# Two chunks of a delta-rule recurrence inverted one by one instead of as a pair, with a new order of all instructions

## The chip, the cores and the metric

The kernel runs on one core of one Trainium2 chip. Its time is the device time of one execution, in microseconds (us); before the change the median of three executions is 238.32 us (238.15 to 238.89). Five engines work side by side, each through its own queue in order: TensorE (PE, matmul), VectorE (DVE), ScalarE (ACT), GpSimd (POOL) and SyncE (SP, which only issues DMAs here). They meet at semaphores.

## The reference

Four batches of eight heads run a gated delta rule over 768 steps with 48 features; its output, 3072 tokens of 384 features, goes through a dense layer of 2048, a softplus and a second dense layer back to 384.

```python
q, k, v, beta, g                       # (4, 8, 768, 48); beta (4, 8, 768)
k_n = k / (norm(k, axis=-1) + 1e-6)
for t in range(768):                   # state (4, 8, 48, 48), zero at first
    y[t] = g[t] * (q[t] @ state)
    state += beta[t] * outer(k_n[t], v[t] - k_n[t] @ state)
x = y.transpose(0, 2, 1, 3).reshape(3072, 384)
out = softplus(x @ w_in) @ w_out       # w_in (384, 2048), w_out (2048, 384)
```

## The kernel before

**Tiling.** The 768 steps are cut into 12 chunks of 64. Within a chunk the recurrence is solved in matrix form: with the gram matrix of the chunk's keys and beta a triangular matrix of 64 by 64 is made for each of the 32 heads, inverted, and the state goes from chunk to chunk by a few matmuls. Chunk by chunk there are these stages, each an *item* of the program:

- load k, q, v, g (SP, in two halves of 192 KB each); square and sum the keys (ksq, red), take the root (sqrt for chunks 0 to 3, pow on GpSimd for the others), scale or cast the keys (kmul, cast), transpose them on TensorE (trs) and evict them (kev, qev);
- gram matrices on TensorE (gram; gramd makes only the diagonal blocks), evicted as kk (kkc, kd) and, masked, as mt (mask);
- the *inversion* of the diagonal blocks (below), then its *join*: xmm, xs, tmm, td2 and zmm make the inverse of the whole 64 by 64 matrix out of the inverses of the 16 by 16 blocks;
- the *chain*, which carries the state from chunk to chunk: ks (keys times state), w (v minus that), umm, u1, zu, u2, smm, s (the new state), and for the output qs, ymm, y, ytr, xt;
- the *dense* layers: g1 (w_in, L992) with softplus on ScalarE (L1004), then g2 (w_out, L1019), eviction (o) and store. Chunks 0, 1, 10 and 11 are dense one by one with 256 columns to a matmul, the others in pairs with 512.

**The inversion.** Chunks go through it in pairs (GROUPS, [0, 1] to [10, 11]). A transpose on VectorE (ln, L594 or L601) puts one 32 by 32 diagonal block of one head on each of 128 partitions: 32 heads by 2 blocks by 2 chunks are 128 lanes. In each lane two blocks of 16 by 16 are inverted side by side by a product (prep, L641) and 15 steps that depend on each other, each a product (tmp, L661) and a sum (tt, L668) on VectorE or GpSimd. ca and cb put the result into the halves of a masked tile (L683 to L685), and three transposes (st.a, st.c, st.b; L711) bring it back to the layout of the heads in dn, tb and td; tx copies half of tb to the other partitions (L209). For group 0 (DIAGONALS) ln reads the diagonal blocks alone, so it need not wait for the whole gram, but it waits for the keys, norms and blocks of both chunks: lbeta (L577 to L580) makes beta over the square of the norm for the pair at once.

**The order.** Nothing schedules the program: a table written out by hand or by a planner (`_ORDER`) names every item by its number with the engine that runs it, and `emit` goes through it. Each engine runs its items in that order; a buffer of a ring (all PSUM banks are one ring of eight) goes to the item that comes first in the table. Items on an engine that wait hold up all behind them. TensorE has 40 optional *fill* items (four matmuls on the identity, L1049) that the table may place, and places 12 times.

**Before the items** the program makes constants: the identity, masks mk and mx, tiles filled with zero or fixed blocks, and GpSimd issues four small DMAs that bring beta of chunks 0 and 1 lane by lane into beta_l (L179).

## Time and profile before

| What | Value |
|---|---|
| median of three executions | 238.32 us (238.15 to 238.89) |
| the profiled execution, its own time | 240.57 us |
| its span, first to last instruction | 238.9 us |
| mean granted clock of TensorE | 0.941 |
| TensorE busy | 217.7 us (91%) |
| VectorE, ScalarE, GpSimd busy | 170.6, 146.8, 114.7 us |
| read from and written to HBM | 25.26 MB, 4.72 MB |

Lines of timelines read: start and length in us, engine, line of the kernel, operation, output<-input without buffer numbers, shapes, the count of instructions merged into the row, and in brackets the idle time before it with what ended it. Lines of stretches read: the stretch, its length, then for TensorE, its weight loads, VectorE, ScalarE and GpSimd the busy us with the number of instructions, then the granted clock, the busy share of the DMA engines and GB/s; with one line of the kernel picked, TensorE's matmuls and weight loads alone. A busy TensorE is not one at its peak, because matmuls are pipelined and their ends are modelled.

### The profile page before, as it was taken

What the parts mean: (1) busy time and instruction counts of PE and PEld (TensorE: products, weight loads), DVE (VectorE), ACT (ScalarE), POOL (GpSimd) and SP (SyncE); (2) the same over time, 40 slices, a digit from 0 to 9 for tenths busy, and PEclk for the clock granted to TensorE, in tenths of its full rate; (3) what the DMA queues carried; (4) which work ended last, traced back from release to release, by engine and by line L of the source; (5) the groups of instructions that cost most, each with busy time, mean ns of one, the idle gap of its engine ahead of it and who ended that gap; (6) DMA issues with size and microseconds to landing.
All of it is one profiled execution on the core that took longest, in us unless ns stands there. A gap on an engine that the chain in (4) does not pass through costs nothing.

```text
span 238.9 us, 11420 instructions
## 1 busy us (share of the span) xinstructions
PE 217.7 (91%) x5016; PEld 141.2 (59%) x5016; DVE 170.6 (71%) x374; ACT 146.8 (61%) x293; POOL 114.7 (48%) x203
## 2 busy tenths in 40 slices
...
PEclk9997955599999958999999999999999999999999
...
GB/s 100 201 210 152 204 130 157 178 187 199 145 144 137 175 180 149 119 136 139 152 164 162 75 79 63 135 139 48 21 20 71 82 69 21 68 22 16 19 53 95
DMA packets 86833, 27.57 MB, mean 115 GB/s; under 512 B 77048, under 2 KB 86776, under 8 KB 86784
## 3 DMA queue, kind: packets, MB, share of 16 engines
...
q0 software_dynamic: 3840, 3.17, 8.8%
...
q14 instruction: 10, 0.08, 0.1%
HBM read 25.26 MB, written 4.72 MB: 126 GB/s over the span
## 4 chain that ended last, share of the span: by engine, by line
PE 72%; POOL 8%; DVE 6%; ACT 5%; issue 4%; DMA 3%; SPq 1%; DVEq 0%; POOLq 0%; ACTq 0%
PE d L992 26%; PE d L1019 22%; PE d L513 3%; PE d L939 3%; DMA f<-in_k_dram 3%; POOL tt L668 3%; PE d L829 2%; PE d L451 2%; POOL tmp L661 2%; PE d L419 2%; PE d L1049 2%; PE d L966 2%; PE d L883 2%; PE d L792 2%; DVE mt L495 2%
## 5 line engine op out<-in xcount | busy, mean ns | idle before, releaser
L1019 PE MATMUL d<-w_out,ga 128*128 128x384 f16 x384 | 70.0, 327 | 0.0
L992 PE MATMUL d<-xt,w_in 128*128 128x512 f16 (+1 forms) x384 | 69.0, 330 | 0.0
L1004 ACT ACTIVATE ga<-d 128x512 f16<-128x512 f32 x96 | 52.8, 604 | 12.7 <-PE d L992 10.8
L992 PEld LDWEIGHTS <-w_in 128*128 128x128 f16 x384 | 35.9, 99 | 22.2 <-issue 0.3
L1019 PEld LDWEIGHTS <-ga 128*128 128x128 f16 x384 | 34.9, 98 | 22.0 <-issue 1.1
L661 POOL TENSOR_TENSOR tmp<-nn,tt 128x78 f32<-128x78 f32 (+7 forms) x58 | 20.6, 356 | 16.3 <-DVE tt L668 12.5
L370 POOL TENSOR_TENSOR nv<-nv,half_c 128x16 f32<-128x16 f32 x8 | 23.5, 2933 | 9.1 <-DVE nv L359 9.0
L668 POOL TENSOR_TENSOR tt<-tt,tmp 128x78 f32<-128x78 f32 (+7 forms) x58 | 22.6, 390 | 4.5
L207 ACT ACTIVATE kqt<-d 128x1024 f16<-128x1024 f16 x18 | 18.3, 1023 | 9.1 <-PE d L451 7.6
L495 DVE TENSOR_TENSOR mt<-d,mask 128x256 f16<-128x256 f32 x48 | 19.0, 414 | 3.3 <-PE d L513 2.9
L207 ACT ACTIVATE osb<-d 128x384 f32<-128x384 f32 x15 | 7.3, 489 | 21.9 <-PE d L1019 21.8
L207 ACT ACTIVATE u<-d 128x384 f16<-128x384 f32 x29 | 13.5, 492 | 11.7 <-PE d L896 5.9
L641 POOL TENSOR_TENSOR nn<-ln,beta_l 128x256 f32<-128x256 f16 x9 | 7.5, 854 | 23.1 <-DVE ln L624 23.0
L953 DVE TENSOR_TENSOR yg<-d,f 128x384 f16<-128x384 f32 x24 | 12.7, 547 | 5.9 <-PE d L939 4.1
L1049 PE MATMUL d<-ident 128*128 128x512 f16 x48 | 14.9, 459 | 1.7 <-DVE ident L195 1.7
L209 DVE CAST u<-d 128x384 f16<-128x384 f32 x19 | 10.2, 552 | 7.3 <-PE d L896 4.0
L209 DVE COPY osb<-d 128x384 f32<-128x384 f32 x9 | 5.0, 552 | 14.0 <-PE d L1019 14.0
L513 PE MATMUL d<-kqt 48*64 48x128 f16 (+1 forms) x448 | 11.6, 229 | 2.8 <-ACT kqt L207 1.3
L869 DVE TENSOR_TENSOR w<-f,d 128x384 f16<-128x384 f32 x22 | 11.3, 539 | 3.1 <-PE d L829 2.7
L927 DVE TENSOR_TENSOR s<-s,d 128x384 f16<-128x384 f16 x20 | 10.7, 547 | 3.0 <-PE d L913 2.9
L209 POOL COPY tx<-tb 64x512 f16<-64x512 f16 x8 | 4.9, 607 | 16.1 <-DVE tb L711 7.4
L359 DVE TENSOR_REDUCE nv<-f 128x16 f32<-128x768 f32 x12 | 11.3, 941 | 1.4 <-POOL f L350 1.4
(117 smaller groups left out, 368.9 us busy)
## 6 DMA issues: line engine op xcount, KB each, us to landing
...
```

The costliest lines, as they stand in the source:

```text
L207: nc.scalar.activation(o, x, AF.Copy, scale=float(sign))
L209: ENG[en].tensor_copy(o, x)
L370: nc.gpsimd.tensor_tensor(nvs(), nvs(), half_c[:, :NU], ALU.pow)
L495: nc.vector.tensor_tensor(mt[c][m].ap[:, NP * p : NP * p + NP], gb[m].ap.rearrange("p (i b) -> p i b", i=NP)[:, :, n : n + C], mask[:, Non ...
L513: nc.tensor.matmul(gb[m].ap.rearrange("p (i b) -> p i b", i=NP)[HALF[r], i, lo:hi], x[:, :C], x[:, lo:hi],)
L661: ENG[en].tensor_tensor(t, nn.ap[:, :, j : j + 1, j + 1 :].broadcast_to([P, 2, w, n]), tt.ap[:, :, :w, j : j + 1].broadcast_to([P, 2, w, n ...
L668: ENG[en].tensor_tensor(rows, rows, t, ALU.add)
L953: lambda en, m=m: nc.vector.tensor_tensor(heads(yg.ap, m), hd(yp[m].ap), heads(gf.ap, m), ALU.mult),
L992: nc.tensor.matmul(hp.ap[:, n * b : n * b + n], w_in[:, j, f * P : (f + 1) * P], xt.ap[:, j, t0 : t0 + n], start=(j == 0), stop=(j == 2),)
L1004: lambda en, hp=hp, o=gb: nc.scalar.activation(o.ap, hp.ap, AF.Softplus),
L1019: nc.tensor.matmul(op.ap[:, :DM], b.ap[:, col + c0 : col + c0 + 128], w_out[:, f, :], start=(f == 0), stop=(f == NF - 1),)
L1049: nc.tensor.matmul(hp.ap, ident, ident[:, None, :].broadcast_to([P, 4, P]))
```

## The change

Group 0 is no longer inverted as a pair. A new function, solo, does it for chunk 0 and again for chunk 1, and a pair's code (inverse) is left to the other five groups; the join is a function of its own that both call. In solo a lane holds one 16 by 16 block of one head: 32 heads by 4 blocks of one chunk are 128 lanes. The transpose (ln1) then moves 256 words instead of 512, a selection (pick1) and a shorter lbeta are added for each chunk, each step's product and sum have half the elements, and there are 30 steps instead of 15. The two halves of a lane's result are masked by mz and mk, the two transposes back (st.a, st.b) have the size they had, the third is gone, and tx copies from td. Beta of chunks 0 and 1 comes in eight DMAs of half the size into beta_s. Each chunk has its own kd (one buffer, so chunk 1's follows chunk 0's) and its own td. Everything else is the same work, but `_ORDER` is written anew for all items, so the place and often the engine of an item differ throughout; 11 fills are placed instead of 12.

```diff
+    mz = pool.tile([P, 2], F32, name="mz")
+    mb = pool.tile([P, 1], F32, name="mb")
+    beta_s = pool.tile([P, 2, 16], F32, name="beta_s")
...
+    r_kd = ring("kd", 1, [P, NU, HC], F16)
...
-            nc.gpsimd.dma_start(
-                out=beta_l[l0 : l0 + 32, 0], in_=bt[:2, :, HC * x : HC * x + HC]
-            )
+            for c in range(2):
+                nc.gpsimd.dma_start(
+                    out=beta_s[l0 : l0 + 32, c],
+                    in_=bt[c, :, HC * x : HC * x + HC].rearrange("u (b k) -> b u k", b=2),
+                )
...
+    def solo(c, cl, kk):
+        nl, bl, nv = Buf(r_nl), Buf(r_bl), nv_of[c]
+        kd, ln, nn, tt, tmp = kd_of[c], Buf(r_ln), Buf(r_n), Buf(r_t), Buf(r_tmp)
...
+        bl_it = add("lbeta", tag, "D", lbeta, deps=[nv_it[c]], bufs=[nv, nl, bl])
...
+        l1 = add("ln1", tag, "D", lnt, deps=kd_it[c], bufs=[kd, ln])
...
+        l1 = add("pick1", tag, "D", pick, deps=[l1], bufs=[ln])
+        prev = add("clear", tag, "GD", lambda en: ENG[en].memset(tt.ap[:, 0], 0.0), bufs=[tt])
...
+        def step(en, j):
+            n, w = 15 - j, j + 1
...
+            t = tmp.ap[:, : n * w].rearrange("p (c i) -> p c i", c=w)
+            ENG[en].tensor_tensor(
+                t,
+                nn.ap[:, 0, j : j + 1, j + 1 :].broadcast_to([P, w, n]),
+                tt.ap[:, 0, :w, j : j + 1].broadcast_to([P, w, n]),
+                ALU.mult,
+            )
+            rows = tt.ap[:, 0, :w, j + 1 :]
+            ENG[en].tensor_tensor(rows, rows, t, ALU.add)
+
+        prev = add("prep", f"{tag}.0", en0, prep, deps=[l1, prev, bl_it], bufs=[ln, nn, bl])
+        for j in range(15):
+            prev = add("step1", f"{tag}.{j}", en0, lambda en, j=j: step(en, j),
+                       deps=[prev], bufs=[nn, tt, tmp], size=(15 - j) * (j + 1))
...
+        ta_it = add("st", f"{tag}.a", "D", lambda en: lanes_out(dn.ap, ta.ap, 0, 1),
+                    deps=ca, bufs=[ta, dn], size=512)
+        td_it = add("st", f"{tag}.b", "D", lambda en: lanes_out(td.ap, rows(), 2, 2),
+                    deps=cb, bufs=[t1, td], size=512)
...
+        if gi in DIAGONALS:
+            for cl, c in enumerate(cs):
+                solo(c, cl, kk_of[gi])
+            return
...
 _ORDER = """
-S25 S26 D227 S34 S33 D6 D11 A176 D173 A9 A1 G169 D170 D0 A171 G5 A197 A12 P129 P152 P164 P132 P162
+S25 S26 A6 A12 G0 G2 G14 G266 G11 G4 A27 A7 A169 D1 D228 D10 D173 S33 S35 S34 D170 P150 P160 P162
```

Three places of the new order, as the instructions stand on their engine (line of that kernel, operation, output<-input with buffer numbers, shape). First GpSimd, around the end of the first inversion; before, the last step of the pair, the copy tx, a weight DMA and the first chain's w:

```order
L661 TENSOR_TENSOR tmp_115<-nn_113,tt_117 128x56
L668 TENSOR_TENSOR tt_117<-tt_117,tmp_115 128x2x14x2
L661 TENSOR_TENSOR tmp_115<-nn_113,tt_117 128x30
L668 TENSOR_TENSOR tt_117<-tt_117,tmp_115 128x2x15
L209 COPY tx_123<-tb_122 64x512
L327 DMA w_in<-in_moe_w_in_dram 128x3x512
L861 TENSOR_TENSOR w_131<-f_76,nv_92 128x384
```

and in the change, from chunk 1's product to the copy tx of chunk 0 (its own last step is three rows above):

```order
L696 TENSOR_TENSOR nn_117<-ln_115,bl_99 128x256
L707 TENSOR_TENSOR tt_120<-nn_117,tt_120 128x15
L712 TENSOR_TENSOR tmp_119<-nn_117,tt_120 128x28
L719 TENSOR_TENSOR tt_120<-tt_120,tmp_119 128x2x14
L712 TENSOR_TENSOR tmp_119<-nn_117,tt_120 128x39
L719 TENSOR_TENSOR tt_120<-tt_120,tmp_119 128x3x13
L712 TENSOR_TENSOR tmp_119<-nn_117,tt_120 128x48
L719 TENSOR_TENSOR tt_120<-tt_120,tmp_119 128x4x12
L712 TENSOR_TENSOR tmp_119<-nn_117,tt_120 128x55
L719 TENSOR_TENSOR tt_120<-tt_120,tmp_119 128x5x11
L217 COPY tx_127<-td_129 64x256
L335 DMA w_in<-in_moe_w_in_dram 128x3x512
```

The copy that the join of chunk 0 needs now follows the first five steps of chunk 1, and the first weight DMA, which stood among the pair's steps, follows the copy.

Second VectorE, around the transpose ln that opens the inversion of chunks 2 and 3 (kk_98 before, kk_101 in the change); before:

```order
L211 TENSOR_SCALAR kk_98<-d_168 128x4x64
L953 TENSOR_TENSOR yg_145<-d_171,f_75 128x8x48
L495 TENSOR_TENSOR mt_111<-d_168,mask 128x256
L953 TENSOR_TENSOR yg_145<-d_174,f_75 128x8x48
L601 STREAM_TRANSPOSE ln_112<-kk_98 128x1024
L380 RECIPROCAL nv_93<-nv_93 128x16
L869 TENSOR_TENSOR w_133<-f_82,d_173 128x384
L869 TENSOR_TENSOR w_131<-f_82,d_174 128x384
```

and in the change (L592 is xs of chunk 1, L217 its td2):

```order
L503 TENSOR_TENSOR mt_114<-d_173,mask 128x256
L367 TENSOR_REDUCE nv_97<-f_84 128x16
L503 TENSOR_TENSOR mt_111<-d_178,mask 128x256
L219 TENSOR_SCALAR kk_101<-d_179 128x4x64
L592 TENSOR_TENSOR xs_128<-d_176,mk 128x16x16
L592 TENSOR_TENSOR xs_128<-d_172,mk 128x16x16
L503 TENSOR_TENSOR mt_114<-d_178,mask 128x256
L217 CAST td_130<-d_174 128x8x2x16
L219 TENSOR_SCALAR kk_101<-d_175 128x4x64
L503 TENSOR_TENSOR mt_113<-d_175,mask 128x256
L797 STREAM_TRANSPOSE ln_115<-kk_101 128x1024
```

The transpose stood ahead of w of chunk 1 and now stands behind that chunk's w, its two transposes back, its xs and its td2.

Third TensorE, in the chain of chunk 2 (zu ends, then smm); before, one of the pieces of the second dense layer stands between:

```order
L896 MATMUL d4_172<-u163_137,z2_130 64x48
L1019 LDWEIGHTS ga9_158
L1019 MATMUL d7_175<-w_out_73,ga9_158 128x384
L1019 LDWEIGHTS ga15_164
L1019 MATMUL d7_175<-w_out_73,ga15_164 128x384
L913 LDWEIGHTS kn2_88
L913 MATMUL d1_169<-u164_138,kn2_88 64x48
```

and in the change zmm of chunk 3 follows zu at once:

```order
L1015 LDWEIGHTS z2_134
L1015 MATMUL d5_177<-u163_141,z2_134 64x48
L1015 LDWEIGHTS z2_134
L1015 MATMUL d6_178<-u162_140,z2_134 64x48
L631 LDWEIGHTS kk1_101
L631 MATMUL d1_173<-td2_131,kk1_101 64x32
```

From xmm of chunk 2 to ytr of chunk 3 there stood eight such pieces, one piece of the first layer and a fill; in the change there are four pieces of the second layer and neither of the others.

396 lines of the change are left out of this document (230 added, 166 removed).

## The prediction

> **What bounds the kernel now.** I read the page's totals first, then a table of busy time in five stretches that I cut at milestones of TensorE, then the chain of waits, and last the timelines of the engines from 0 to 91 us. The page:
>
> ```profile
> span 238.9 us, 11420 instructions
> ...
> PEclk9997955599999958999999999999999999999999
> ```
>
> The granted clock of TensorE is given in 40 slices of 5.97 us: it is down in the first third alone, worst in the sixth to eighth slice (30 to 48 us) and the fifteenth (84 to 90). The stretches (time, then busy us of each engine with its instructions, clock, DMA share, GB/s):
>
> ```profile
> 0.00:44.20 44.20, 31.65 (x795) 20.97 (x796) 37.57 (x97) 31.68 (x61) 26.48 (x50) 0.80 1.01 165
> 44.20:65.60 21.40, 20.84 (x340) 15.73 (x336) 15.69 (x39) 16.52 (x31) 15.65 (x27) 0.94 1.18 178
> 65.60:91.00 25.40, 21.63 (x711) 15.34 (x710) 20.04 (x42) 13.43 (x28) 15.51 (x28) 0.87 0.83 158
> 91.00:235.00 144.00, 143.54 (x3180) 89.19 (x3176) 97.33 (x200) 84.66 (x174) 57.01 (x100) 1.00 0.45 84
> 235.00:238.90 3.90, 0.00 (x0) 0.00 (x0) 0.00 (x0) 0.48 (x1) 0.00 (x0) 0.88 0.38 90
> ```
>
> The cuts are these starts on TensorE: the first dense matmul (chunk 0, 256 columns), the join of chunk 2 (xmm), and the first dense matmul of chunks 2 and 3 (512 columns):
>
> ```profile
> 44.18 1.46 PE L992 MATMUL d<-xt,w_in 128*128 128x256 f16 x6
> 65.61 0.43 PE L741 MATMUL d<-dn,kk 64*64 64x32 f16 x32
> 91.02 4.76 PE L992 MATMUL d<-xt,w_in 128*128 128x512 f16 x21
> ```
>
> From 91.0 to 235.0 TensorE idles 144.00 - 143.54 = 0.46 us at full clock: that stretch is pure work, and the same work after the change. So the kernel's time is the moment M at which chunks 2 and 3 become dense, plus 144.0, plus a tail of 3.9. An edit in the first 91 us is worth what it moves M, and nothing else; starting chunk 0's dense work earlier is worth nothing by itself, because chunks 0 and 1 together hold too little of it to last until M.
>
> **The change, step by step.**
>
> *The inversion of chunk 0.* Now the two chunks are inverted as one pair:
>
> ```profile
> 13.65 0.19 DVE L579 TENSOR_TENSOR bl<-beta_l,nl 128x32 f32<-128x32 f32 x1
> 14.18 1.04 DVE L594 STREAM_TRANSPOSE ln<-dn 128x512 uint32<-128x512 uint32 x1
> 15.26 0.76 DVE L641 TENSOR_TENSOR nn<-ln,bl 128x256 f32<-128x256 f16 x2
> 22.20 0.28 DVE L661 TENSOR_TENSOR tmp<-nn,tt 128x128 f32<-128x128 f32 x1
> ...
> 18.81 0.41 POOL L661 TENSOR_TENSOR tmp<-nn,tt 128x120 f32<-128x120 f32 x1 [2.41 <-DVE tt L668]
> 19.30 0.41 POOL L668 TENSOR_TENSOR tt<-tt,tmp 128x120 f32<-128x120 f32 x1
> 27.50 0.25 POOL L661 TENSOR_TENSOR tmp<-nn,tt 128x30 f32<-128x30 f32 x1
> 27.83 0.26 POOL L668 TENSOR_TENSOR tt<-tt,tmp 128x30 f32<-128x30 f32 x1
> ...
> 1.64 2.65 POOL L179 DMA_DIRECT2D beta_l<-in_beta_dram  x4 [0.27 <-issue]
> beta_l<-in_beta_dram POOLq DMA_DIRECT2D x4, 4.0 KB, 4.8
> ```
>
> The pair's steps end at 27.83 + 0.26 = 28.1. In the change chunk 0 no longer waits for chunk 1's load, but for its beta: the four DMAs cost GpSimd 0.66 us each to issue (2.65 / 4), eight cost 5.3; the seventh is the last that chunk 0 needs, is issued at 1.64 + 6 x 0.66 = 5.6 to 6.3, and lands 4.8 later, at 11. Then two products of 0.19, half a transpose (0.5), the selection (0.4 at most), one product for nn (0.38): 12.6. Step 1 stands on VectorE (0.5 with the hop), the other 13 pairs on GpSimd. Their size halves but not their time: 30 elements cost 0.25 and 120 cost 0.41, so 0.20 + 0.0018 per element; 15 to 64 elements cost 0.285 on average, and the two rows at 18.81 and 19.30 stand 0.49 apart, 0.08 more than the first lasts. 26 x (0.285 + 0.08) = 9.5. **End 23.1 instead of 28.1: -5.0.** A bound from below: on VectorE a full-sized one is 0.28, so nothing on the chip makes these steps much shorter than that; from above: GpSimd's full cost, 26 x 0.49 = 12.7, end 26.3.
>
> *From there to the first dense matmul.* 28.1 to 44.2 is 16.1 us now. Two rows of GpSimd (a copy tx that the join needs, and two products for nn):
>
> ```profile
> 31.66 0.60 POOL L209 COPY tx<-tb 64x512 f16<-64x512 f16 x1 [3.58 <-DVE tb L711]
> 46.81 2.17 POOL L641 TENSOR_TENSOR nn<-ln,beta_l 128x256 f32<-128x256 f16 x2
> ```
>
> The copy ends 31.66 + 0.60 - 28.1 = 4.2 after the steps now. The change puts it behind two short clears, chunk 1's product (1.1, half of 2.17) and first five steps (nine instructions of 0.365: 3.3); with the copy itself it ends about 5.1 after the steps. The rest of the chain to the first dense matmul keeps its instructions. So 16.1 + 0.9 = 17, and the first dense matmul starts at about 40: 4 us of lead. Its weights are issued later than now (GpSimd's queue has them behind chunk 1's steps), and I take them as just in time.
>
> *Chunk 1 behind it, and the transpose for chunks 2 and 3.* Now one set of steps serves both chunks; in the change GpSimd begins chunk 1's when chunk 0's are done, and they end near 38: 23.1, the clears and the product (1.4), eleven steps on GpSimd at 0.73 (8.0), the copy (0.4), four weight DMAs at the 0.66 of beta's (2.6), and 2.5 for four steps on VectorE with two hops there and back. What matters is who waits there: VectorE's queue. Now the transpose (ln) that opens the inversion of chunks 2 and 3 stands ahead of chunk 1's subtraction w; in the change it stands behind the whole join of chunk 1 (two transposes, two xs, td2):
>
> ```profile
> 42.30 1.92 DVE L601 STREAM_TRANSPOSE ln<-kk 128x1024 uint32<-128x1024 uint32 x1
> 44.45 1.02 DVE L869 TENSOR_TENSOR w<-f,d 128x384 f16<-128x384 f32 x2
> 29.44 1.08 DVE L711 STREAM_TRANSPOSE dn<-ta 128x512 uint32<-128x512 uint32 x1
> 27.59 1.40 DVE L495 TENSOR_TENSOR mt<-d,mask 128x256 f16<-128x256 f32 x4
> 62.99 0.92 DVE L359 TENSOR_REDUCE nv<-f 128x16 f32<-128x768 f32 x1
> ```
>
> From 38 VectorE has two w (1.0), two transposes (2.2), some ten masks, evictions and xs (0.35 each, 1.40 / 4: 3.5) and a reduction (0.9): 7.6 us of work, so the transpose cannot start before 45.6. It also waits for three other engines on the way (ScalarE's masked copies ahead of the transposes, GpSimd's tx copies and TensorE's tmm ahead of td2). I give each hop 0.8, an estimate from the 0.6 to 1.4 that evictions and copies last in the rows here: the transpose starts at about 48 instead of 42.3, **+5.7**. At 2 us for each it is 52, the other bound.
>
> *The inversion of chunks 2 and 3.* Now from the transpose at 42.30 to the last step:
>
> ```profile
> 59.69 0.26 POOL L668 TENSOR_TENSOR tt<-tt,tmp 128x30 f32<-128x30 f32 x1
> 62.03 1.07 DVE L711 STREAM_TRANSPOSE tb<-tw 128x512 uint32<-128x512 uint32 x1
> 64.31 1.00 DVE L711 STREAM_TRANSPOSE dn<-ta 128x512 uint32<-128x512 uint32 x1
> ```
>
> That is 17.6 us. In the change eight of the steps are on VectorE instead of six, at 0.28 for GpSimd's 0.41, and VectorE has the inversion's rows closer together; against that GpSimd multiplies kn of chunk 4 ahead of nn. I take 16.3, end 64.3, **+4.4**. Behind the last step xmm starts 5.7 later now, because the transpose that it reads (64.31) stands behind another (62.03) and the reduction (62.99); in the change it comes first, so 2.5 remains: 66.8 against 65.6, **+1.2**.
>
> *Between xmm of chunk 2 and M.* This is 25.4 us now and the largest term. TensorE's own dense work and a filler stand in this chain:
>
> ```profile
> 65.60:91.00 25.40, 6.49 (x33) 2.60 (x32) 0.87 0.83 158
> 65.60:91.00 25.40, 0.83 (x6) 0.51 (x6) 0.87 0.83 158
> 65.60:91.00 25.40, 1.33 (x4) 0.31 (x4) 0.87 0.83 158
> ```
>
> (first the second dense layer, eight pieces of four matmuls, then a first-layer piece, then the filler). In the change four pieces of the second layer remain in this stretch and neither of the others: 3.2 + 0.8 + 1.3 = 5.4 us less. Not all of it was on the chain, since chunk 2's and 3's evictions also ran meanwhile; I take two thirds, **-3.5**, of bounds 0 and -5.4. So 66.8 + 21.9 = 88.7.
>
> *The clock.* The half clock of 84 to 91 ended just as the dense stretch began. The change has no filler there, so TensorE is emptier ahead of M. If the clock comes back later, dense work runs at half speed. The shortest spell is the one in this row:
>
> ```profile
> 18.00:24.00 6.00, 4.95 (x49) 3.17 (x48) 5.67 (x18) 5.63 (x10) 3.26 (x6) 0.72 1.04 151
> ```
>
> Its loss is 6.0 x (1 - 0.72) = 1.7 us. I take +0.7 of bounds 0 and 1.7. The Trainium skill ("TensorE: Matmul & The Clock Gate", Part 1) says that the clock returns after one busy window of about 3.4 us that does not start with the work; by that the price is at most half of 3.4, and the row, a loss of 1.7, agrees.
>
> **The sum.** M moves by +1.2 - 3.5 + 0.7 = -1.6, to 89.4; the 144.0 and the 3.9 stay. The profiled execution took 240.57 (span 238.9 and 1.7 around it) and would take 239.0; it lies 2.25 above the median of the runs shown, 238.32, so the median becomes **236.7**.
>
> **Rivals.** *The steps save nothing:* the inversion of chunks 2 and 3 still takes 17.6 (1.3 more than assumed), so M moves by -0.3: 238.0. For it: GpSimd carries pow and kn before nn in both orders. Against: two more steps on VectorE at 0.28 instead of 0.41.
>
> *A slower one: the delay of the transpose decides.* If the 25.4 us are set by evictions and not by the dense pieces between them, the -3.5 is nothing, and with 17.6 for the inversion M moves by 1.2 + 1.3 + 0.7 = +3.2: 241.5. For it: chunks 2 and 3 run one after the other through five evictions each. Against: TensorE was busy 21.63 of the 25.4. It decides once the stretch behind xmm lasts longer than 91.0 - 66.8 = 24.2 us.
>
> *Another slower one: the start.* A copy on VectorE lasted ten times as long as its like while GpSimd issued DMAs and cleared tiles:
>
> ```profile
> 3.49 2.46 DVE L209 COPY kk<-pat 128x512 f16<-128x512 f16 x1
> 5.88 0.27 DVE L209 COPY td<-pat 128x512 f16<-128x512 f16 x1
> 4.25 1.00 POOL L183 MEMSET tw<- 128x1024 uint32 x1
> ```
>
> Four DMAs more make that 2.65 us longer; the cast of chunk 0 waits behind the copy, all else follows, and M moves by -1.6 + 2.6 = +1.0: 239.3. The Trainium skill ("SBUF — State Buffer", Who interferes with whom) has a rule that speaks for it: the two engines share a port pair that one instruction holds alone. The row agrees; that it would last until GpSimd's clears end, no row shows.
>
> *Faster than forecast:* the transpose starts at its lower bound, 45.6, and the clock is back in time: M moves by -1.6 - 2.4 - 0.7 = -4.7: 233.6. For it: VectorE is idle 44.20 - 37.57 = 6.6 us ahead of 44.2 now, so there is room. Against: three engines have to be on time at once.
>
> **Numbers.** A measurement of this kernel can't tell less than 0.3%, 0.7 us, from no change. Forecast 0.40; faster than it 0.10; nothing saved 0.17; the transpose decides 0.23; the start 0.10. Faster 0.50, same 0.17, slower 0.33. The forecast's own range is 235.0 to 237.6; the signs are mixed, so the whole range goes from 232.5, below the fast rival, to 241.6, the price of the slow one.
>
> **What would show it.** Chunk 0's last step near 23, the first dense matmul near 40, the transpose for chunks 2 and 3 near 48, xmm of chunk 2 near 67, the first 512-column matmul near 89, and behind that 144 us with TensorE full. I am wrong if the last of these is not so (new idle behind M), if the steps on GpSimd cost what the full-sized ones do, or if the first 512-column matmul comes after 91.

## The result and the profile after

The changed kernel takes 245.23 us (median; 244.53 to 248.49) against 238.24 us (237.24 to 238.89) for the kernel before: a ratio of 1.029, 95% interval 1.024 to 1.034. It is **slower by 7.0 us**; the forecast was 236.7, and the range ended at 241.6. Medians and ranges here and below are over all executions, while the ratios use only those in the faster of the two states that a kernel's executions fall into, so a ratio can differ a little from that of the medians. The two profiled executions lie closer together, 245.14 and 240.57 us, spans 243.2 and 238.9: those 4.3 us are what the traces can explain. Of the other 2.7 most is the 2.3 us by which the kernel before lay above its median (238.24) when it was profiled.

The page of the changed kernel, its span, the granted clock in 40 slices and the shares of the chain that ended last:

```profile
span 243.2 us, 11463 instructions
...
PEclk9995769999999959999999999999999999999999
...
PE 48%; POOL 14%; DVE 12%; DMA 10%; ACT 6%; issue 6%; SPq 3%; ACTq 0%; POOLq 0%
```

The same row of the chain in the kernel before:

```profile
PE 72%; POOL 8%; DVE 6%; ACT 5%; issue 4%; DMA 3%; SPq 1%; DVEq 0%; POOLq 0%; ACTq 0%
```

The clock is no worse. TensorE's share of the chain fell by 24 points, and that of GpSimd, VectorE and DMA rose: the chain that ended last runs more through the small work and the loads. The stretches, cut at 44 and 66 us and at M (the start of the first 512-column dense matmul), first of the changed kernel and then of the one before (busy us of TensorE, its weight loads, VectorE, ScalarE and GpSimd):

```profile
0.00:44.00 44.00, 30.96 (x669) 18.39 (x670) 35.12 (x92) 29.83 (x60) 35.20 (x87) 0.84 1.18 170
44.00:66.00 22.00, 18.78 (x431) 13.24 (x429) 16.89 (x38) 12.53 (x27) 12.89 (x21) 1.00 0.91 143
66.00:95.06 29.06, 23.87 (x774) 18.57 (x772) 26.34 (x57) 18.70 (x39) 22.32 (x32) 0.88 0.83 157
```

```profile
44.00:66.00 22.00, 21.44 (x389) 16.24 (x382) 16.29 (x39) 17.01 (x33) 16.25 (x28) 0.94 1.17 181
66.00:91.02 25.02, 21.25 (x685) 14.97 (x678) 19.66 (x42) 13.14 (x28) 15.11 (x28) 0.87 0.84 157
```

M moved from 91.02 to 95.06, by 4.0 us; behind M both kernels take the same (243.2 - 95.06 = 148.1 and 238.9 - 91.02 = 147.9). So the whole loss of the span lies ahead of M. TensorE idles 22.00 - 18.78 = 3.2 us between 44 and 66, where it had idled 0.56 and in a second profile of the kernel before 0.02; between 66 and M it idles 5.2 instead of 3.8.

What TensorE does about 66 us, with the VectorE rows it depends on. The changed kernel (xt: the dense input of chunk 1; s: the state after chunk 1; `d<-s,kqt` at 71.48: ks, with which chunk 2's chain begins; `d<-dn,kk`: xmm of chunks 2 and 3; L1111 and L1138: the dense layers):

```profile
63.23 0.56 DVE L217 COPY xt<-d 128x768 f16<-128x768 f16 x1 [0.60 <-PE d L1085]
66.21 0.54 DVE L1046 TENSOR_TENSOR s<-s,d 128x384 f16<-128x384 f16 x1
69.58 0.21 DVE L863 TENSOR_TENSOR tt<-tt,tmp 128x30 f32<-128x30 f32 x1
...
64.19 5.41 PE L1111 MATMUL d<-xt,w_in 128*128 128x256 f16 x48
69.44 2.11 PE L1138 MATMUL d<-w_out,ga 128*128 128x384 f16 x12
71.48 0.44 PE L948 MATMUL d<-s,kqt 48*64 48x48 f16 x32
72.60 0.69 PE L580 MATMUL d<-dn,kk 64*64 64x32 f16 x64
95.06 3.20 PE L1111 MATMUL d<-xt,w_in 128*128 128x512 f16 x14
```

The kernel before:

```profile
52.14 0.56 DVE L209 COPY xt<-d 128x768 f16<-128x768 f16 x1 [0.40 <-PE d L966]
65.51 0.54 DVE L927 TENSOR_TENSOR s<-s,d 128x384 f16<-128x384 f16 x1
...
57.69 2.14 PE L992 MATMUL d<-xt,w_in 128*128 128x256 f16 x18
59.66 1.46 PE L1019 MATMUL d<-w_out,ga 128*128 128x384 f16 x8
61.60 4.07 PE L1019 MATMUL d<-w_out,ga 128*128 128x384 f16 x24
65.97 0.83 PE L992 MATMUL d<-xt,w_in 128*128 128x256 f16 x6
66.73 0.44 PE L829 MATMUL d<-s,kqt 48*64 48x48 f16 x32
```

Before, xt of chunk 1 was there at 52.70, and TensorE worked without a gap from 57.69 to ks, mostly at four of chunk 1's eight first-layer pieces and at chunk 0's second layer; the other four had run ahead of that. The state was ready at 66.05; ks of chunk 2 started at 66.73, when its turn came in TensorE's queue, 1.12 us behind xmm of chunk 2. Now xt of chunk 1 is there at 63.79, 11.1 us later. Its eight first-layer pieces stand in TensorE's queue ahead of ks in both kernels; in the changed one three pieces of the second layer stand ahead of it too, and xmm of chunks 2 and 3 stands behind it. The state is ready at 66.75, only 0.7 later than before, but ks starts at 71.48, 4.75 later than before and 4.73 behind its state. From 44.00 to ks it was 22.73 us before, of which TensorE was busy 22.17; it is 27.48 now, of which TensorE is busy 24.26. So of the 4.75 about 2.7 are TensorE's idling, in a stretch in which chunk 1's dense work was not there yet, and 2.1 are the three pieces (the row at 69.44).

### The profile page after: what moved, and what is told of

It reads as the page before. It is cut to its first block, busy times and chain, and to the rows that moved or that the text cites. A ratio compares the mean times of both kernels' runs of the same rounds, so it can differ in the third digit from the quotient of the medians.

```text
span 243.2 us, 11463 instructions
## 1 busy us (share of the span) xinstructions
PE 216.7 (89%) x5012; PEld 139.3 (57%) x5012; DVE 172.2 (71%) x376; ACT 149.1 (61%) x313; POOL 127.2 (52%) x237
## 4 chain that ended last, share of the span: by engine, by line
PE 48%; POOL 14%; DVE 12%; DMA 10%; ACT 6%; issue 6%; SPq 3%; ACTq 0%; POOLq 0%
PE d L1111 20%; PE d L1138 17%; DMA f<-in_k_dram 5%; POOL tt L863 4%; POOL tmp L856 4%; DMA w_out<-in_moe_w_out_dram 3%; SPq L310 3%; PE d L521 2%; PE d L610 2%; DVE ln L797 2%; ACT ga L1123 2%; DMA f<-in_q_dram 1%; PE d L948 1%; POOL tt L719 1%; POOL nv L378 1%
## 5 line engine op out<-in xcount | busy, mean ns | idle before, releaser
L1138 PE MATMUL d<-w_out,ga 128*128 128x384 f16 x384 | 71.2, 327 | 1.4 <-DMA w_out<-in_moe_w_out_dram 1.4
L1111 PE MATMUL d<-xt,w_in 128*128 128x512 f16 (+1 forms) x384 | 67.0, 326 | 2.3 <-ACT xt L215 2.0
L1111 PEld LDWEIGHTS <-w_in 128*128 128x128 f16 x384 | 36.1, 98 | 25.5 <-issue 2.5
L1138 PEld LDWEIGHTS <-ga 128*128 128x128 f16 x384 | 34.6, 98 | 22.6 <-issue 1.8
L856 POOL TENSOR_TENSOR tmp<-nn,tt 128x120 f32<-128x120 f32 (+7 forms) x49 | 18.7, 383 | 16.8 <-DVE tt L863 12.9
L215 ACT ACTIVATE u<-d 128x384 f16<-128x384 f32 x36 | 17.0, 494 | 13.9 <-PE d L1015 7.8
L378 POOL TENSOR_TENSOR nv<-nv,half_c 128x16 f32<-128x16 f32 x8 | 23.6, 2948 | 1.9 <-DVE nv L367 1.7
L863 POOL TENSOR_TENSOR tt<-tt,tmp 128x120 f32<-128x120 f32 (+7 forms) x49 | 20.3, 414 | 3.8
L215 ACT ACTIVATE kqt<-d 128x1024 f16<-128x1024 f16 (+1 forms) x17 | 16.4, 977 | 2.1 <-PE d L427 0.9
L215 ACT ACTIVATE osb<-d 128x384 f32<-128x384 f32 x19 | 9.1, 491 | 9.9 <-PE d L1138 9.2
L215 ACT ACTIVATE z<-d 128x256 f16<-128x256 f32 x19 | 6.9, 386 | 12.3 <-PE d L631 12.3
L215 ACT ACTIVATE kk<-d 128x256 f16<-128x256 f32 x30 | 11.0, 386 | 5.5 <-PE d L521 5.3
L217 DVE CAST u<-d 128x384 f16<-128x384 f32 x12 | 6.6, 554 | 9.1 <-PE d L1002 4.1
L948 PE MATMUL d<-s,kqt 48*64 48x48 f16 x704 | 10.4, 191 | 1.1 <-DVE s L1046 1.0
```

What stands on the lines that cost most here:

```text
L215: nc.scalar.activation(o, x, AF.Copy, scale=float(sign))
L378: nc.gpsimd.tensor_tensor(nvs(), nvs(), half_c[:, :NU], ALU.pow)
L856: ENG[en].tensor_tensor(t, nn.ap[:, :, j : j + 1, j + 1 :].broadcast_to([P, 2, w, n]), tt.ap[:, :, :w, j : j + 1].broadcast_to([P, 2, w, n ...
L863: ENG[en].tensor_tensor(rows, rows, t, ALU.add)
L948: nc.tensor.matmul(hd(o[m].ap)[HALF[r], pi], kq(c, r, pi)[FEAT[m], off : off + C], s0[r].ap[FEAT[m], pi], **start(pi),)
L1111: nc.tensor.matmul(hp.ap[:, n * b : n * b + n], w_in[:, j, f * P : (f + 1) * P], xt.ap[:, j, t0 : t0 + n], start=(j == 0), stop=(j == 2),)
```

## The experiments

My first theory after the result was the late pair (called **P**): the transposition ln for chunks 2 and 3 starts at 51.25 instead of 42.30, the inversion ends at 69.79 instead of 59.95, so xmm and M come late. The rival, **Q**, became sharper on the way: chunk 1's output comes late, and with it TensorE's dense work, which then stands in the way of chunk 2's chain. Each ratio below is against the kernel before as measured in the same round; its median lay between 238.98 and 241.94 us there, so times of different rounds compare only loosely. Milestones of all runs in us (ln: transposition of chunks 2 and 3; steps: end of their inversion; xt: end of chunk 1's copy; ks: of chunk 2; xmm: the first of the two of chunks 2 and 3, chunk 2's except in g1, w1, w2 and o1, where chunk 3's comes first):

| run | ln | steps | xt | ks | xmm | M | M - ks |
|---|---|---|---|---|---|---|---|
| before | 42.30 | 59.95 | 52.70 | 66.73 | 65.61 | 91.02 | 24.3 |
| b1 before, again | 42.46 | 59.63 | 53.16 | 66.99 | 65.87 | 90.13 | 23.1 |
| after | 51.25 | 69.79 | 63.79 | 71.48 | 72.60 | 95.06 | 23.6 |
| c1 weights early | 52.01 | 69.67 | 63.66 | 71.35 | 72.47 | 95.12 | 23.8 |
| e1 steps on GpSimd | 50.82 | 69.40 | 64.62 | 72.31 | 73.44 | 95.44 | 23.1 |
| p1 ports apart | 50.20 | 68.57 | 62.56 | 70.25 | 71.38 | 94.11 | 23.9 |
| s1 no second steps | 49.61 | 68.12 | 62.11 | 69.80 | 70.93 | 94.41 | 24.6 |
| f1 mended | 52.64 | 68.67 | 63.55 | 71.24 | 72.37 | 94.90 | 23.7 |
| d1 ln early | 47.60 | 75.77 | 69.69 | 77.38 | 78.50 | 100.84 | 23.5 |
| d2 ln early | 47.36 | 71.36 | 67.44 | 75.13 | 76.96 | 99.58 | 24.5 |
| d3 chain and ln early | 48.77 | 70.46 | 62.61 | 77.84 | 78.97 | 101.86 | 24.0 |
| b2 before, ln late | 52.04 | 66.93 | 55.25 | 75.76 | 74.64 | 100.21 | 24.5 |
| t1 after, no pair steps | 51.81 | none | 63.95 | 71.64 | 72.77 | 95.37 | 23.7 |
| t2 before, no pair steps | 42.74 | none | 53.28 | 67.11 | 65.99 | 91.83 | 24.7 |
| g1 t1, pair moved ahead | 51.16 | none | 62.49 | 74.71 | 65.56 | 95.72 | 21.0 |
| a1 solo in the old order | 54.31 | 72.23 | 67.08 | 80.85 | 79.72 | 102.68 | 21.8 |
| o1 solo, searched order | 53.08 | 74.34 | 72.94 | 77.25 | 79.48 | 105.53 | 28.3 |
| o2 pair, searched order | 51.05 | 74.57 | 66.54 | 77.16 | 78.28 | 101.93 | 24.8 |
| w1 window re-ordered | 48.92 | 70.12 | 64.76 | 67.11 | 72.61 | 97.74 | 30.6 |
| w2 window re-ordered | 49.27 | 75.12 | 68.64 | 82.05 | 78.82 | 103.26 | 21.2 |

Chunk 2's xmm starts at 73.76 in w1, 80.86 in w2 and 80.92 in o1; in g1 the first two matmuls of chunk 3's start at 65.56 and all the others, chunk 2's with them, at 66.02.

In the diffs below a row is one engine's queue at that place, by the items' names: the item, then its chunk or pair, then its piece or step (`ks:2` is ks of chunk 2, `step:2.7` step 7 of chunks 2 and 3, `g1:1.4` and `g2:1.1.4` pieces of chunk 1's first and second dense layer). Items between those of a row may be left out of it.

### b1: the kernel before, once more

No edit. 

> The kernel before, profiled once more, because the profiled execution shown of it took 240.57 us, 2.3 above its median. If that execution was an ordinary one with a late first stretch, this one shows the first 512-column dense matmul at 89 to 90 us instead of 91.0 and a time near 238; if it was ordinary work slowed everywhere, the stretch behind it is shorter than 147.9 instead and the first 512-column matmul stays at 91.

239.72 us in one run, M 90.13. A second profile of the same kernel differs by 0.9 us in M; the other milestones agree to 0.5. Differences of M under 1 us say nothing here.

### c1: the dense weights earlier

```diff
 GpSimd: wload:w1.1
+GpSimd: wload:w1.2 wload:w1.3
```

> The changed kernel with the two last DMAs of w_out (w1.2 and w1.3) moved on GpSimd's queue from 47.4 and 52.1 us to right behind the first two, near 42.4, in the 3.1 us in which GpSimd waits for the transpose of chunk 1. Theory 'weights': TensorE's waits for w_out at 56.4 (0.51 us) and 60.1 (0.90) and what stands behind them (ymm, y, ytr, xt of chunk 1, and with xt the step 2.7 on VectorE) set the time; without them the first 512-column matmul comes about 2 us earlier, at 93, and the time is near 243. Theory 'transpose' (the late transpose ln for chunks 2 and 3 sets the time): the waits for w_out go, ln stays at 51 and the time moves by less than 1 us from 245.2.

244.79 us (244.5 to 244.84), ratio 1.019 (1.009 to 1.029). TensorE's two waits for w_out, 1.4 us together in the changed kernel, are gone, and M stays (95.12): late weights are not the cause.

### e1 and p1: the pair's steps 7 and 8 on GpSimd; a collision taken apart

In the changed kernel VectorE's copy ca of chunk 1 lasts 1.97 us, where others of its size take 0.4, beside GpSimd's squares of chunk 4:

```profile
42.16 1.97 DVE L731 TENSOR_SCALAR ta<-tt,mz 128x256 f16<-128x256 f32 x1
42.40 1.49 POOL L358 TENSOR_TENSOR f<-f 128x768 f32<-128x768 f32 x1
```

```diff
 e1
-VectorE: step:2.7 step:2.8
+GpSimd:  step:2.7 step:2.8
 p1
-GpSimd:  ksq:4
+ScalarE: kev:k2.0 ksq:4
-ScalarE: ca:1.0
+VectorE: ca:1.1 ca:1.0
```

> The changed kernel with steps 7 and 8 of the pair 2/3 on GpSimd instead of VectorE, where they stood behind chunk 1's xt (GpSimd idled 3.51 us for them and VectorE spent 1.3 on them). In the runs so far the first 512-column matmul (M) followed the pair's last step by 25.1 to 25.4 us in every version of the new order. Theory 'queue' (VectorE's queue, with chunk 1's chain in it, sets the pair's last step, and this sets M): steps 7 and 8 end on GpSimd at 62.3 + 2.0 = 64.3 instead of 65.6, the last step, which then waits only for chunk 1's s and the reduction on VectorE (67.6), ends near 68.6 instead of 69.8, M is near 93.9 instead of 95.1 and the time near 244.0. Theory 'chain' (the state's chain, s of chunk 1 and the keys of chunk 2, sets M, and the steps only keep pace): M stays at 95.0.

> The changed kernel with ksq of chunk 4 on ScalarE, in its idle time near 39.6, instead of on GpSimd at 42.4, and both of chunk 1's ca on VectorE. VectorE's ca took 1.97 us there instead of 0.41, from 42.16 to 44.13, and GpSimd's ksq ran from 42.40 to 43.89. Theory 'ports' (a VectorE instruction of this kind stands still while GpSimd works, and such stretches lie on the path to the transpose): ca takes 0.4, or ends at once when GpSimd's two DMA issues end at 42.4, the transposes of chunk 1 begin near 43.5 instead of 44.85, ln near 50 instead of 51.25, M 1 us earlier. Against it: ca still takes 1.5 or more beside the DMA issues alone, or the time is unchanged because other waits take the place.

e1: 246.09 us (245.11 to 246.37), ratio 1.026 (1.019 to 1.034), M 95.44: nothing gained, although a 3.5 us gap in the steps is closed (GpSimd's steps lie 0.5 us apart, VectorE's 0.3, and the power for chunk 5 comes later). p1: 245.11 us (244.55 to 245.58), ratio 1.023 (1.017 to 1.029). Both ca together take 0.78 there, ln comes 1.05 earlier, and M 0.95 earlier; the time did not move. The collision is real, but taking it apart moved M by hardly more than the 0.9 of two profiles of one kernel.

### s1: no second set of steps

```diff
         def step(en, j):
             n, w = 15 - j, j + 1
+            if c == 1 and j:
+                return
```

Steps 1 to 14 of chunk 1's inversion are left out, in solo. 

> The changed kernel without chunk 1's steps 1 to 14: all 28 instructions are left out (the inverse of chunk 1's blocks is then wrong), everything else stays in its place. It prices the second inversion by itself. Theory 'solo': chunk 1's part that came out of the steps ends near 33 instead of 41, the transpose ln, which stands behind chunk 1's join on VectorE, comes at 45 to 47 instead of 51.25, and M at 90 to 92; the time is 240 to 242, about that of the kernel before. Theory 'order' (VectorE's other work and the loads, not the steps, hold ln): ln moves by less than 2 us and the time stays above 243.

244.14 us in one run. M 94.41: **in this order 30 steps instead of 15 cost 0.65 us of M, no more than two profiles of one kernel differ.** ln, xt and ks came 1.6 to 1.7 us earlier. The two copies that follow the steps stood elsewhere in their queues anyway:

```profile
39.85 0.53 ACT L731 ACTIVATE tb<-tt,mz 128x256 f16<-128x256 f32 x1
41.40 0.44 DVE L733 TENSOR_SCALAR ta<-tt,mz 128x256 f16<-128x256 f32 x1
```

ScalarE took up the first behind the keys of chunks 2 and 3, VectorE the second at 41.40, 0.8 earlier than with the steps. So what follows the steps kept its place, and most of chunk 1's delay with it; that the steps cost nothing in any order is not shown.

### f1: the small mends together

p1's edit, e1's, the weights of c1 behind the copy tx, and chunk 4's reduction and power earlier.

```diff
+GpSimd:  pow:4 behind wload:w1.1; kmul:4.0 wload:w1.2 wload:w1.3 behind tx:1.0
+VectorE: red:4 behind step1:1.14
+TensorE: gram:3.0 behind xmm:1
```

> The changed kernel with five mends together: ksq of chunk 4 on ScalarE and both ca on VectorE (ports apart); the reduction and pow of chunk 4 moved ahead, so that pow (2.94 us) fills GpSimd's idle time from 43.9 to 47.0 instead of standing between chunk 1's tx and the pair's product nn; kn of chunk 4 and the last two w_out DMAs behind tx; the last gram of chunk 3 two dense pieces earlier on TensorE; steps 7 and 8 of the pair on GpSimd. Theory 'queue': ln near 48.5, the pair's last step near 64 to 65, M near 89.5 to 90.5, time 239 to 241, within 1% of the kernel before. Theory 'chain': ln and steps come earlier, but M by less than 2 us, time above 243.

245.91 us (243.98 to 250.51), ratio 1.024 (1.015 to 1.032). ln was expected near 48.5 and came at 52.64, 1.4 later than in the changed kernel. The pair's inversion shrank from 18.5 us behind ln to 16.0, but xt of chunk 1 stayed (63.55), and so did ks (71.24) and M (94.90). Here P and Q part for the first time, though by little: the steps end 1.1 us earlier and M moves 0.16, where two profiles of one kernel differed by 0.9 in M.

### d1, d2 and d3: the transposition earlier in the changed kernel

Part of VectorE's queue in d2; d1 and d3 differ in what else was brought forward with it (d3 also chunk 1's chain).

```diff
-VectorE: xs:1.1 xs:1.0 mask:3.00 td2:1.0 kkc:3.01 mask:3.01 ln:2 eps:4 clear:4 mask:2.10 pick:2
+VectorE: ca:1.1 mask:2.00 red:4 st:1.a st:1.b mask:3.11 ln:2 pick:2 xs:1.1 xs:1.0 mask:3.10
```

> The changed kernel with the transpose ln for chunks 2 and 3 moved ahead on VectorE: the four grams of chunks 2 and 3 stand together on TensorE, their evictions stand ahead of chunk 1's ca and cb1, and ln and its selection come right behind the two transposes of chunk 1, ahead of its xs and td2 (and GpSimd's clear, diag, prep with it, pow:4 into GpSimd's idle time near 44). Theory 'transpose': ln starts near 46 instead of 51.25 and the first 512-column matmul comes 3 to 5 us earlier, at 90 to 92; the time is 240 to 242. Theory 'solo' (two inversions one behind the other cost it, wherever the transpose stands): chunk 1's join and chain come later by what the transpose takes (2 us), and the time stays within 1 us of 245.2. Theory 'weights': no gain either, since w_out comes no earlier.

> The changed kernel, both solo inversions in it, with the transpose ahead as in the run before, without what went wrong there: on TensorE xmm of chunk 1 stands ahead of the dense pieces that waited for banks, the filler comes later, and steps 7 to 10 of the pair are on GpSimd, so no step stands behind chunk 1's xt; all four w_out DMAs are issued together. Theory 'late transpose': ln near 47, the pair's last step at 64 to 66, M at 89 to 91.5, time 238.5 to 241, level with the kernel before. Theory 'chain' (chunk 1's chain on VectorE and TensorE sets the pair's end): the last step stays at 68 or later, M above 93, time above 242.

> The changed kernel, both solo inversions in it, with the stretch from 39 to 65 us ordered anew on all engines, so that neither of the two things that compete for VectorE waits for the other: the grams of chunks 2 and 3 in front, the transpose ln right behind chunk 1's two transposes, chunk 1's chain (umm to s) ahead of the dense pieces on TensorE and ahead of the pair's later steps on VectorE, reduction and pow of chunk 4 behind tx, steps 7 to 14 of the pair on VectorE behind s of chunk 1, ksq of chunk 4 on ScalarE, all w_out DMAs together. Theory 'order' (solo costs little; what the change loses is that transpose and chain come late): ln at 46 to 48, the pair's last step at 62 to 65, M at 88 to 91, time 237 to 241. Theory 'two things at once' (with solo, chunk 1's join and chain fall into the stretch in which the pair 2/3 needs VectorE, and one of them has to wait in any order): the last step stays at 67 or later or xmm of chunk 2 waits for the chain, M at 94 or above, time 243 or above.

d1: 250.82 us, ratio 1.045 (1.036 to 1.054); d2: 249.37, 1.041 (1.034 to 1.049); d3: 251.43, 1.054 (1.045 to 1.063). ln came at 47.4 to 48.8, earlier than in the changed kernel, and M **later** by 4.5 to 6.8 us. In d1 and d2 the order that let ln pass delayed chunk 1's chain (xt 69.69 and 67.44; in d1 TensorE waited 2.30, 1.03 and 1.60 us for VectorE's masking of grams, at a granted clock of 0.53 between 42 and 60), and the pair's last steps stood on VectorE behind chunk 1's own u2, xt and s, so that even they ended no earlier. In d3 the power of chunk 4 (2.94 us) and the wait for it held the pair's first product instead, and other work in TensorE's queue held ks until 77.84, although the state was ready at 63.54. In none of them did an early transposition gain anything. But the steps ended at 70.46 to 75.77 against 69.79, so the early inversion that P asks for never came about, and these runs do not test P.

### a1, o1, o2: one part of the change alone

The solo inversion in the order of the kernel before (by hand), the solo inversion in an order searched anew from the durations of these traces, and the pair in an order by the same search. VectorE's queue about the transposition:

```diff
 a1 (solo)
+VectorE: kkc:3.10 kkc:3.01 kkc:3.00 mask:3.00 ln:2 eps:4 w:1.1 w:1.0 clear:4 diag:4 pick:2
 o1 (solo)
+VectorE: mask:3.10 mask:2.00 w:1.0 mask:3.01 ln:2 diag:2 pick:2 w:1.1
 o2 (pair)
+VectorE: mask:3.10 eps:4 y:0.1 y:0.0 ln:2 w:1.0 pick:2 w:1.1
```

> The solo inversions of the change in the order of the kernel before: everything behind the first dense work stands as before, chunk 0's steps are on GpSimd, chunk 1's first five steps run beside them on VectorE and its last ten follow on GpSimd, so the transpose ln for chunks 2 and 3 keeps the place that it had, ahead of the first w of chunk 1. Theory 'transpose' or any theory that blames the new order: ln starts at 42 to 45 and the time is within 1.5 us of the kernel before, 237 to 240. Theory 'solo': about as slow as the change, 243 to 246, with ln at 42 to 45 all the same.

> The changed kernel with all its instructions, both solo inversions among them, and only the order of the items up to the first dense work of chunks 2 and 3 written anew on every engine: a search moved one item at a time and kept what made the first 512-column matmul (M) earlier, with each item's duration taken from the traces shown so far. The search was run in the same way on the kernel before (the next run). Theory 'order' (what the change lost lies in the order that came with it, not in the solo inversions): M comes at least 6 us earlier than the change's 95.1, at 89 or before, and the time is 239 or less, level with the kernel before or under it. Theory 'solo': M stays above 92 and the time above 242.

> The kernel before, one pair inversion for chunks 0 and 1, with the order of the same stretch written anew by the same search. It is the partner of the run ahead of it: two inversions, one kind of order. Theory 'order': the two lie within 1.5 us of each other, since the pair's and the solos' steps both hide. Theory 'solo': the pair is 3 us or more faster than the solos, because each solo brings its own ca, cb, transposes and tx and a second set of 15 steps. If neither order is better than the one by hand, both are slower than 240 and the runs say nothing on the inversions.

a1: 254.72 us, ratio 1.059 (1.048 to 1.070); ln was expected at 42 to 45 and came at 54.31, with xt at 67.08, so this order does not give back the early transposition. o1: 264.39, 1.094 (1.083 to 1.105). o2: 267.39, 1.116 (1.107 to 1.125). As the expectation of o2 provides, a pair that the search makes 28 us slower than the order it had says that the search is poor, not which inversion is better. Whether an equally well fitted order would make solo level stays open.

### w1 and w2: only 39 to 76 us re-ordered

```diff
 w1
-TensorE: g1:1.14 g2:1.1.0 g2:1.1.4 g2:1.1.8 ks:2 g2:1.0.0 xmm:2 xmm:3
+TensorE: g1:1.14 g1:1.6 trs:q5 g2:1.1.0 g2:1.0.0 xmm:3 g2:1.1.4 xmm:2
 w2
+TensorE: g1:1.12 g2:1.1.4 xmm:3 g2:1.1.8 g2:1.0.4 tmm:3 xmm:2 trs:k5.0 ks:2
```

> The changed kernel, both solo inversions in it. Up to 39 us every engine keeps the change's order, loads included (the run before this one lost its time there: TensorE at 0.59 of its clock between 20 and 40 us, the first dense matmul at 51.8). Only what stands between 39 and 76 us is ordered anew on TensorE, VectorE, ScalarE and GpSimd, so that ln comes near 48, the chain of chunk 1 before the pair's later steps, and four of chunk 1's dense pieces behind xmm of chunk 3. Theory 'order' (the time that the change lost lies in the order of this stretch): xt of chunk 1 near 58 instead of 63.2, the pair's last step near 64 instead of 69.8, M at 89 to 92, the time 238 to 242. Theory 'solo' (with solo, no order of this stretch is much better, since VectorE has to do chunk 1's join and the pair's inversion in it): M at 94 or later, 244 or more.

> The same with another order of the same stretch (both grams of chunk 3 first, both ca of chunk 1 on VectorE, xt of chunk 1 earlier, its dense pieces in another order), so that the answer does not hang on one order. Same forecasts: by 'order' the pair's last step near 63 to 65, M at 89 to 92 and 238 to 242; by 'solo' M at 94 or later and 244 or more.

w1: 249.44 us, ratio 1.049 (1.032 to 1.066). w2: 253.21, 1.061 (1.051 to 1.071). xt near 58 and M at 89 to 92 were expected of both; xt came at 64.76 and 68.64, and M at 97.74 and 103.26. w1 is the one run of the changed code with ks as early as before (67.11): it stands behind three of chunk 1's eight first-layer pieces instead of all. But xmm came at 72.61 (chunk 3's) and 73.76 (chunk 2's), behind all eight. An early ks without an early join gains nothing.

### b2: the transposition late in the kernel before

```diff
-VectorE: mask:3.00 y:0.0 ln:2 eps:4 w:1.1 w:1.0 diag:4 pick:2
+VectorE: u2:1.1 y:1.0 y:1.1 ln:2 pick:2 mask:3.11 xt:1 step:2.7
```

> The kernel before, pair inversion and order as they were, with one thing moved: the transpose ln for chunks 2 and 3 and its selection stand on VectorE behind the y of chunk 1 instead of ahead of chunk 1's w. No inversion of chunk 1 by itself is in it. ln starts at 49.5 to 51.5 us instead of 42.4, about where the change has it (51.25). Theory 'late transpose' (what the change lost is the place of this transpose, whatever put it there): the pair's last step and the first 512-column matmul (M) come 6 to 9 us later, M at 96 to 99, time 245 to 248, no faster than the change. Theory 'solo' (the two inversions themselves cost the time): M moves by less than 3 us, since TensorE's dense work fills the wait, time 239 to 242.

250.26 us (247.18 to 254.62), ratio 1.040 (1.024 to 1.055). It looks like P: ln at 52.04, M at 100.21. The rows say how:

```profile
61.71 0.29 DVE L661 TENSOR_TENSOR tmp<-nn,tt 128x128 f32<-128x128 f32 x1 [6.46 <-POOL tt L668]
67.31 0.54 DVE L927 TENSOR_TENSOR s<-s,d 128x384 f16<-128x384 f16 x1
...
67.90 0.97 PE L513 MATMUL d<-kqt 48*64 48x128 f16 x16 [4.71 <-DVE s L927]
68.81 5.90 PE L1019 MATMUL d<-w_out,ga 128*128 128x384 f16 x24
75.76 0.44 PE L829 MATMUL d<-s,kqt 48*64 48x48 f16 x32
```

The pair's later steps stand on VectorE ahead of chunk 1's state s, and VectorE waits 6.46 us for GpSimd's half of them. The first half of s comes at 67.31 instead of 60.33, and TensorE, at a gram of chunk 4, waits 4.71 us for it. 24 matmuls of dense work stand behind that gram and ahead of xmm and ks. So ks starts 9.0 us later, M 9.2. A late transposition can cost a lot in that order, through what is queued behind it.

### t1 and t2: no steps for the pair at all

```diff
         def step(en, j):
             n, w = 15 - j, j + 1
+            if gi == 1 and j:
+                return
```

Steps 1 to 14 of chunks 2 and 3 are left out, of the changed kernel (t1) and of the kernel before (t2). 

> The changed kernel without steps 1 to 14 of the pair 2/3 (28 instructions left out, so the inverses of chunks 2 and 3 are wrong); everything else stays in its place, the transpose ln with it. It asks how far M would come if that inversion cost nothing but its transposes. Theory 'transpose' (the late ln, through the pair's steps, sets M): M comes 6 us or more earlier, at 89 or before, and the time is 239 or less. Theory 'queue' (chunk 1's xt at 63.2, 11 us later than before, and its dense pieces ahead of xmm of chunk 2 on TensorE hold M as well): the steps end early, but xmm of chunk 2 still comes at 71 or later, M at 93 or later, time 243 or more.

> The kernel before without the same 28 instructions of the pair 2/3. Theory 'transpose': M was set by the pair's steps there as well and comes 6 us or more earlier, at 84 or before. Theory 'queue': the steps leave little slack there too, and xmm of chunk 2, behind the dense pieces of chunks 0 and 1, moves by less than 3 us, M stays at 87 or later.

t1: 246.68 us in one run, M 95.37. t2: 241.42 beside 241.94 for the kernel before, M 91.83. **Without the steps of the inversion that P holds to be the bound, and with all else in its place, neither kernel gains.** One caveat, from t1's rows (the inverse's first half, the power for chunk 5, the transposition of that half, ks):

```profile
66.64 0.78 DVE L882 TENSOR_SCALAR ta<-tt,mx 128x256 f16<-128x256 f32 x2
66.81 3.07 POOL L378 TENSOR_TENSOR nv<-nv,half_c 128x16 f32<-128x16 f32 x1 [9.20 <-DVE nv L367]
70.44 1.01 DVE L908 STREAM_TRANSPOSE dn<-ta 128x512 uint32<-128x512 uint32 x1
71.64 0.44 PE L950 MATMUL d<-s,kqt 48*64 48x48 f16 x32
```

What follows the steps kept its place: VectorE's transposition stands behind a reciprocal that waits for GpSimd's power, so xmm could not have come before 71.5. The next run takes that away.

### g1: the pair's join moved ahead as well

t1, and behind chunk 1's xt at once ca, cb, the transpositions, xmm, xs, tmm and td2 of chunks 2 and 3; on TensorE two of chunk 1's pieces ahead of xmm instead of all eight:

```diff
-TensorE: g1:1.2 g1:1.4 g1:1.6 g1:1.0 g1:1.10 g1:1.12 g1:1.8 g1:1.14 g2:1.1.0 g2:1.1.4 g2:1.1.8 ks:2 g2:1.0.0 xmm:2 xmm:3
+TensorE: g1:1.2 g1:1.4 xmm:3 xmm:2 tmm:3 tmm:2 g1:1.6 g1:1.0 g1:1.10 g1:1.12 g1:1.8 g1:1.14 g2:1.1.0 g2:1.1.4 g2:1.1.8 ks:2
```

> The run with steps 1 to 14 of chunks 2 and 3 left out (so their inverse is not the reference's) moved nothing, because what follows the steps stayed in its old places: xmm of chunk 2 still came at 72.77, behind 5.4 us of chunk 1's first dense layer on TensorE, behind that layer's softplus on ScalarE and behind GpSimd's 3.07 us power on VectorE. Here the steps are left out as there, and what follows them (the two inverse halves, the transposes, xmm, xs, tmm of chunks 2 and 3) is placed right behind chunk 1's xt, with only two of chunk 1's eight first-layer pieces ahead of xmm on TensorE. Theory A, the chain through xmm of chunk 2 sets the start of the 512-column work: xmm at about 67, that start 4 to 6 us earlier than 95.4 (89 to 91), time 239 to 242. Theory B, TensorE's own work sets it: what idles up to the late xt of chunk 1 is gone for good, and pieces that are pushed behind xmm are done later for the same time; xmm at about 67 as well, but the start at 93.5 or later and the time 244.5 to 247.

248.88 us (246.24 to 250.3), ratio 1.039 (1.029 to 1.050).

```profile
65.56 0.20 PE L580 MATMUL d<-dn,kk 64*64 64x32 f16 x2 [1.19 <-DVE mt L503]
66.02 0.77 PE L580 MATMUL d<-dn,kk 64*64 64x32 f16 x62 [0.26 <-DVE s L1048]
68.73 4.10 PE L1113 MATMUL d<-xt,w_in 128*128 128x256 f16 x36
72.67 2.11 PE L1140 MATMUL d<-w_out,ga 128*128 128x384 f16 x12
74.71 0.44 PE L950 MATMUL d<-s,kqt 48*64 48x48 f16 x32
95.72 2.55 PE L1113 MATMUL d<-xt,w_in 128*128 128x512 f16 x11
```

xmm came at 65.56 to 66.02, 6.6 to 7.0 us earlier than in the changed kernel and about as early as in the kernel before, and M at 95.72, no earlier: theory A of this expectation, that xmm and the inversion ahead of it set M by themselves, has fallen, and so has P as it was stated; B's numbers are met. But the run doesn't show that B is the mechanism, since the pieces that were pushed back still stand ahead of ks, which starts 3.2 later. An early xmm with an early ks was not reached.

### What the runs leave

In nine kernels that keep the changed kernel's order on TensorE behind chunk 1's xt (after, c1, e1, p1, s1, f1, d1, d2, t1), ks of chunk 2 starts 7.69 us behind xt's end, the same to the hundredth in all of them. Nothing but TensorE's queue stands between. In d3, where xt came at 62.61, 1.2 earlier than in the changed kernel, other items of that queue came ahead of chunk 1's pieces (70.55), and ks again 7.29 behind the first of these, as in the changed kernel (71.48 - 64.19). M follows ks by 23.1 to 24.8 us in 15 of the 20 rows. The five others: with the pair's join done early (g1) or ks very late (a1, w2) the distance is 21.0 to 21.8; with chunk 2's join later than ks (o1, w1) it is 28.3 and 30.6. In most rows ks and xmm lie about 1.1 us apart, so that this distance cannot tell one from the other. What fits all 20 rows is that **M follows the later of ks and xmm of chunk 2, by 21.0 to 24.7 us**: an early xmm with a late ks (g1) gains nothing, nor an early ks with a late xmm (w1).

So **shown**, in the orders tried, is that none of these sets M alone: the pair's steps, an early xmm, an early ks, the second set of steps, the weights, or the collision. **Read from the traces, but not edited by itself,** is that ks and xmm both stand in TensorE's queue behind chunk 1's late dense work: of the 4.75 us of ks about 2.7 are TensorE's idling ahead of it (1.4 of the 3.2 idle us were the waits for w_out, and where c1 removes them ks moves by only 0.13) and 2.1 the three pieces that now stand ahead of it. **Open** is what an early xt would give: no kernel with solo inversions had xt of chunk 1 before 62.1 (s1), against 52.70 in the kernel before, though w1, w2 and d3 were meant to have it early. Open too is a kernel with both ks and xmm ahead of chunk 1's pieces, which was not tried. No run of the changed code beats the kernel before.

Why xt of chunk 1 is 11.1 us late can be read from TensorE's rows of its chain (umm at `d<-w,td`, the join's zmm at `d<-td,kk`, zu at `d<-u,z`, ymm at `d<-u,mt`), first in the changed kernel:

```profile
51.47 0.44 PE L1002 MATMUL d<-w,td 64*64 64x48 f16 x32
53.25 0.70 PE L631 MATMUL d<-td,kk 64*64 64x32 f16 x32
57.40 0.42 PE L1015 MATMUL d<-u,z 64*64 64x48 f16 x32
60.87 0.62 PE L1058 MATMUL d<-u,mt 64*64 64x48 f16 x28
```

and in the kernel before:

```profile
43.19 0.61 PE L792 MATMUL d<-td,kk 64*64 64x32 f16 x32
45.57 0.63 PE L883 MATMUL d<-w,td 64*64 64x48 f16 x32
47.48 0.42 PE L896 MATMUL d<-u,z 64*64 64x48 f16 x32
49.67 0.69 PE L939 MATMUL d<-u,mt 64*64 64x48 f16 x32
```

umm is 5.9 late. From umm to ymm it now takes 9.4 us instead of 4.1, 5.3 more: zmm came ahead of umm and comes behind it now, so that its eviction, zu and the rest of the chain follow one after another between dense pieces of chunk 0. Before, the pair's common join had chunk 1's inverse ready with chunk 0's, and zmm of chunk 1 (43.19) came right behind chunk 0's chain (its ymm at 39.37).

## Why the prediction was wrong

**Right.** M as the pivot: 148.1 us behind it in the changed kernel (243.2 - 95.06), 147.9 predicted. Chunk 0 did get a lead in its steps: the last ends at 24.25 (23.1 predicted, 28.1 before). Less of it was left at the first dense matmul, which starts at 42.90 (40 predicted, 44.18 before), 18.65 us behind the last step instead of the 17 predicted. From xmm of chunk 2 to M it took 22.5, predicted 21.9. The clock did not cost: 0.88 between 66 and M against 0.87 before, and the 1.7 us that were taken as its upper bound were the loss of the shortest spell, which bounds nothing from above.

**The step that failed** is the term "xmm of chunk 2 +1.2". It measured +7.0 (72.60 instead of 65.61). The rest of the sum, -3.5 + 0.7 = -2.8, measured -2.9 (from 25.4 to 22.5 us), so that M moved by +4.0 instead of -1.6. The path was wrong, and not only the size: xmm was made to follow the pair's inversion alone, with no term for chunk 1's output xt, which moved from 52.70 to 63.79, and none for what stands ahead of ks and xmm in TensorE's queue. Leaving the steps of that inversion out (t1) did not make xmm or M earlier, nor did shortening it (f1); g1 shows that xmm alone can come 6.6 to 7.0 us earlier with the same M. What the changed kernel's trace shows in its place: xmm stands behind ks and chunk 1's late dense pieces. How much of the delay an earlier xt alone would take away stays open.

What led there is the sentence "starting chunk 0's dense work earlier is worth nothing by itself, because chunks 0 and 1 together hold too little of it to last until M". From it I followed chunks 2 and 3 and did not follow chunk 1 past its steps. Dense work that is little must also come in time: TensorE had idled 0.56 us between 44.0 and 66.0 with chunk 1's first-layer pieces and chunk 0's second layer lying there, and with xt 11.1 us later it idles 3.2, and the pieces fall where chunk 2's chain wants TensorE. I had the end of chunk 1's steps at 38 (41.1 measured).

**"Inversion 16.3, end 64.3"**: ln at 51.25 (48 predicted, upper bound 52), inversion 18.5, end 69.79. Its 3.5 us gap, where VectorE's steps 7 and 8 stand behind chunk 1's xt, was the mis-sized term: I had counted two more steps on VectorE as a gain and had not asked what they are queued behind. In the order of t1, f1 and e1 none of this reached M.

**"-3.5" for fewer dense pieces behind xmm**: the stretch did shrink, by 2.9, but what was counted as removed had only moved ahead of xmm and ks. The table of pieces was right; that they cost as much there as they had behind is argued, not shown.

**Smaller terms.** The 23.1 of chunk 0's last step is shown as 12.6 and 26 x (0.285 + 0.08) = 9.5 with step 1's 0.5 between, which add up to 22.6. The product nn ended at 13.66 instead of 12.6, and from there to the last step it took 10.6. Some of GpSimd's half-sized steps took 0.22 us, less than the 0.28 that was given as the least.

**The rivals.** "The delay of the transpose decides" moves M by 3.2, and 4.0 was measured, so it came nearest in number; its mechanism is not what the runs show, since it left the stretch behind xmm at 25.4, which shrank by 2.9, and the transposition's delay by itself is not what M follows. "The steps save nothing" had the inversion at 17.6 (18.5 measured). "The start": VectorE's copies took 0.23 to 0.29 us beside GpSimd's eight DMA issues, none like the 2.46 before, and beta was waited for 0.45 us. The chance of a third for slower was too low because each case was worked out along one chain.

**Weights**: "just in time" was wrong for w_out (1.4 us of waits), and c1 shows that it did not matter.
